# A windowed-attention and mixture-of-experts kernel: one written order for five sequencers, PSUM as eight named banks, shared own values in stage 1

## The chip, the cores and the metric

The kernel runs on one core of one Trainium2 chip. The metric is the device time of one execution in microseconds (us). The engines are TensorE (PE, its weight loads shown as PEld), VectorE (DVE), ScalarE (ACT), GpSimd (POOL) and SyncE (SP, which here only issues DMAs).

## The reference, cut to what matters

Two attention layers follow each other, for 8 batches of 576 positions.

```python
# stage 1: 8 heads of 64, each query sees the 64 positions up to itself
scores = (q @ k.transpose(0, 1, 3, 2)) / 8            # [8, 8, 576, 576]
mask = (rel >= 0) & (rel < 64)
x = softmax(where(mask, scores, -1e9)) @ v            # -> x [8, 576, 512]
# stage 2: 4 experts, each a causal attention with one head of 64; 2 experts per token by a gate
logits = x @ w_gate;  topk, w = best 2 of 4, softmax over the two
for e in range(4):
    q, k, v = x @ wq[e], x @ wk[e], x @ wv[e]
    ye = softmax(causal(q @ k.T / 8)) @ v @ wo[e]     # [8, 576, 512]
    out += (weight of e, 0 where e is not chosen) * ye
```

## The kernel before, in words

Stage 1 works on blocks of 64 positions; five units `d` per batch hold blocks 0-1, 2-3, 4-5, 6-7 and 8 (`UNITS`). `s1_mm` puts the scores of a unit into two PSUM banks, `s1_soft` makes the softmax in the tile `p1` of the unit: masked maximum on DVE (line 183, `tensor_tensor_reduce`, a custom instruction in the trace), exp on ACT (190), normalisation on POOL (198), 32x32 transposes on DVE (203). Stage 2 works on pairs of experts `pr`: `s2_v`, `s2_k`, `s2_q` are projections (lines 224 to 226: each product of fp32r parts is three matmuls), `s2_mm` the scores of half `x` of the rows (357), `s2_soft` and `s2_w` their softmax in `P2[pr]` (375, 379, 418), `s2_turn` the transposes (433), `s2_gate` the gate, `s2_o` the output projection with its copy (595) and store.

Both value products are one routine, `av`: 32x64 tiles of the array, four row groups `r` and two column groups `c`, all matmuls at line 528. A joint call takes the 18 key groups of one `(b, pr)` of stage 2 and units of stage 1 of batch `b+2`: units 0, 1 with `pr` 0, units 2, 3, 4 with `pr` 1. For batches 0 and 1 each unit has a call of its own (`EARLY`). In stage 1 a block `k` takes the values of its own block and of the one before; the first block of a unit needs extra steps, "edge", because its probabilities of the block before lie in its own tile and can't ride with the step "own" of that block, as they do inside a unit (`m` 2: one matmul of 64 columns). Each product of fp32 operands stands in the trace as two matmuls with a weight load each. The result is evicted by pairs: ACT copies to the fp32r high part (554), DVE subtracts it for the low part (555). The stage-2 values come from `VR`, one tile, filled by `s2_rep` with 24 DMAs (16 of `VN`, 8 of `V8`) for each `(b, pr)`, which can start when the `av` before has read `VR`. The values of stage 1 are loaded by `load_v`, 16 DMAs for each third of a batch.

PSUM holds one buffer of four banks, tag `a`, which `s2_mm` (both halves) and `av` take in turn, and four buffers of one bank, tag `s`, for all else (`s1_mm` takes two).

`put` gives each routine a time in units of half a batch, from tables (`EARLY`, `S1POS`, `BPOS`, `APOS`, `POS`, `WPOS`). The calls are sorted by it. Up to 1.0 and from 15.5 on the framework's scheduler orders all engines; between, PE keeps the sorted order (`manual_schedule`) and the framework orders DVE, ACT, POOL and SP.

Of the kernel before, what the change touches and what calls it, by code (L numbers as in the profile page):

```python
# [25 lines left out]
P1BUFS = 4  # L26
EARLY = ((-0.9, -0.7), (-0.8, -0.5), (-0.65, -0.35), (-0.5, -0.2), (-0.35, -0.1),
         (-0.2, 0.1), (0.0, 0.35), (0.3, 0.6), (0.5, 0.8), (0.7, 0.95))
S1POS = (0.04, 0.69, 0.04, 0.38, 0.69)
BPOS = (0.05, 0.7)  # L30
APOS = 0.4
POS = {"KQ1": (-0.2, 0.95), "O": (0.45, 1.3), "V": (-0.5, 0.2), "G": (0.2, 0.2), "KQ0": (0.2, 0.95), "V8": (0.45, 0.55)}
WPOS = (-0.7, -0.3, -0.2, 0.4)
FIXED = (1.0, 15.5)
# [3 lines left out]
def window_attention_moe_attention(ctx: ExitStack, tc: tile.TileContext, qT, kT, vW,  # L38
# [5 lines left out]
    psum = ctx.enter_context(tc.tile_pool(name="psum", bufs=2, space=PSUM))  # L44
# [6 lines left out]
    def banks(name, tag, n=1):  # L51
        return psum.tile([128, n, 512], F32, tag=tag, bufs=1 if tag == "a" else 4, name=name)
# [84 lines left out]
    def split_weights(i):  # L137
# [5 lines left out]
        yield "lo"  # L143
# [10 lines left out]
    S1, P1 = {}, {}  # L154

    def s1_mm(b, d):
        k0, k1 = UNITS[d]
        ps = [psum.tile([128, 2, 2, 128], F32, tag="s", bufs=4, name=f"s1_{b}_{d}_{x}") for x in range(2)]
# [14 lines left out]
    def s1_soft(b, d):  # L173
# [4 lines left out]
        pt = work.tile([128, 2, NP, 128], F32, tag="p1", bufs=P1BUFS, name=f"p1_{b}_{d}")  # L178
        yield "ttr"
        for k in range(n):  # L180
            for p in range(NP):
                own = 64 if k0 + k == 0 else 0
                nc.vector.tensor_tensor_reduce(out=pt[:, k, p, own:], in0=ps[p % 2][:, k, p // 2, own:],  # L183
                                               in1=win[:, own:], scale=-0.125, scalar=3.0e38, op0=OP.add, op1=OP.min,
                                               accum_out=st[:, 0, k, p:p + 1])
        yield "exp"
        for k in range(n):
            for p in range(NP):
                own = 64 if k0 + k == 0 else 0
                nc.scalar.activation(pt[:, k, p, own:], pt[:, k, p, own:], AF.Exp, bias=st[:, 0, k, p:p + 1],  # L190
                                     scale=-1.0, accum_out=st[:, 1, k, p:p + 1])
        yield "norm"
        nc.vector.tensor_scalar_add(st[:, 2, :n], st[:, 1, :n], 1e-9)
        nc.vector.reciprocal(st[:, 2, :n], st[:, 2, :n])  # L194
        for k in range(n):
            for p in range(NP):
                own = 64 if k0 + k == 0 else 0
                nc.gpsimd.tensor_scalar(pt[:, k, p, own:], pt[:, k, p, own:], st[:, 2, k, p:p + 1], 1.0,  # L198
                                        op0=OP.mult, op1=OP.mult)
        yield "turn"  # L200
        for k in range(n):
# [26 lines left out]
    def s2_v(b, j):  # L228
        if j < 4:
            need(("x", b, j), ("w", "v"))  # L230
        else:
            need(("x", b, 4), ("x", b + 1, 4))
        ps = psum.tile([128, 512], F32, tag="s", bufs=4, name=f"v2ps_{b}_{j}")
# [6 lines left out]
        yield "v"  # L240
# [24 lines left out]
    def s2_gate(b, j0, j1):  # L265

        n = j1 - j0
        need("late", *(("v", b, j) for j in range(j0, j1)))
# [4 lines left out]
        tc.keep_in_program_order(nc.vector.tensor_tensor(g4[:, 0], lf, le, op=OP.is_gt))  # L273
# [8 lines left out]
        nc.vector.tensor_sub(gt[:, 1], lg, gs[:, 0, :, None].to_broadcast([128, n, E]))  # L282
# [80 lines left out]
    def s2_soft(b, pr, x):  # L363
# [17 lines left out]
        for k, parts in enumerate(SCORES[x]):  # L381
            for i, key, n, at in parts:
                if i == 1:
                    n = 192
# [350 lines left out]
```

## Time and profile before

| what | value |
|---|---|
| median of 3 runs | 783.1 us (780.98 to 784.85) |
| profiled execution: its own time | 782.28 us |
| its span, first to last instruction | 780.5 us |
| mean granted TensorE clock, as a share of 2.4 GHz | 0.782 |
| busy: PE, PEld, DVE, ACT, POOL | 539.0, 484.1, 406.0, 290.1, 189.7 us |
| first joint `av` starts / last one with stage-1 units ends | 148.3 us / 670 us |

A busy share is an average over stages. PE's time is the span less its idle time, and the idle time has a releaser: what ended it. "issue" as a releaser means that PE waited for nothing that the profile shows.

### The profile page before, as it was taken

What the parts mean: (1) busy time and instruction counts of PE and PEld (TensorE: products, weight loads), DVE (VectorE), ACT (ScalarE), POOL (GpSimd) and SP (SyncE); (2) the same over time, 40 slices, a digit from 0 to 9 for tenths busy, and PEclk for the clock granted to TensorE, in tenths of its full rate; (3) what the DMA queues carried; (4) which work ended last, traced back from release to release, by engine and by line L of the source; (5) the groups of instructions that cost most, each with busy time, mean ns of one, the idle gap of its engine ahead of it and who ended that gap; (6) DMA issues with size and microseconds to landing.
All of it is one profiled execution on the core that took longest, in us unless ns stands there. A gap on an engine that the chain in (4) does not pass through costs nothing.

```text
span 780.5 us, 30957 instructions
## 1 busy us (share of the span) xinstructions
PE 539.0 (69%) x13006; PEld 484.1 (62%) x13006; DVE 406.0 (52%) x1813; ACT 290.1 (37%) x1162; POOL 189.7 (24%) x470
## 2 busy tenths in 40 slices
PE   3358759676596765968478766787578756698775
PEld 2257648566585654857366666766567656587564
DVE  2545546846157362674427563565625844376542
ACT  3334535534135341534215351443504523234210
POOL 2421413423024030241303321032312312021120
PEclk9566778876588695988769685796858878699877
DMA  5654342134343313433235232443324121122332
GB/s 157 190 157 122 85 126 79 44 79 117 80 127 103 106 32 82 134 97 86 78 89 153 72 91 52 112 118 76 107 61 138 58 49 32 32 84 58 85 86 69
DMA packets 81884, 72.30 MB, mean 93 GB/s; under 512 B 14416, under 2 KB 68688, under 8 KB 81744
## 3 DMA queue, kind: packets, MB, share of 16 engines
q1 hardware_dynamic: 81664, 70.19, 33.0%
q8 instruction: 102, 1.67, 0.9%
q14 instruction: 38, 0.31, 0.1%
q10 hardware_dynamic: 80, 0.13, 0.0%
HBM read 41.95 MB, written 9.44 MB: 66 GB/s over the span
## 4 chain that ended last, share of the span: by engine, by line
PE 42%; DVE 15%; issue 13%; ACT 13%; POOL 10%; SPq 4%; DMA 3%; POOLq 0%; ACTq 0%; DVEq 0%
PE o L528 20%; POOL p L198 8%; ACT p L190 8%; DVE p L375 3%; PE s L168 3%; DVE p L433 2%; SPq L82 2%; PE s L357 2%; DVE p L203 2%; DMA k<-in_kT_dram 2%; ACT p L379 2%; PE qps L224 2%; PE kps L224 2%; PE kps L225 2%; PE kps L226 2%
## 5 line engine op out<-in xcount | busy, mean ns | idle before, releaser
L198 POOL TENSOR_SCALAR p<-p,st 128x128 f32<-128x128 f32 (+1 forms) x288 | 99.0, 366 | 291.9 <-DVE st L194 127.7
L528 PE MATMUL o<-p,v 32*64 32x32 f32 (+1 forms) x5504 | 95.4, 279 | 96.2 <-issue 68.2
L528 PEld LDWEIGHTS o<-p,v 32*64 32x64 f32 x5504 | 88.0, 188 | 101.8 <-issue 82.3
L190 ACT ACTIVATE p<-p,st 128x128 f32<-128x128 f32 (+1 forms) x288 | 110.1, 384 | 68.0 <-DVE st L183 62.6
L528 PE MATMUL o<-p,vr 32*64 32x128 f32 (+3 forms) x4224 | 86.6, 302 | 63.3 <-DVE r L375 37.4
L528 PEld LDWEIGHTS o<-p,vr 32*64 32x64 f32 x4224 | 79.8, 166 | 70.1 <-issue 66.2
L554 ACT ACTIVATE xh<-o 128x128 fp32r<-128x128 f32 (+3 forms) x88 | 30.2, 343 | 217.6 <-PE o L528 184.5
L555 DVE TENSOR_TENSOR xl<-o,xh 128x128 fp32r<-128x128 f32 (+3 forms) x88 | 32.7, 371 | 134.0 <-ACT xh L554 133.9
L379 ACT ACTIVATE p<-p,r 128x192 f32<-128x192 f32 (+3 forms) x128 | 77.4, 605 | 65.7 <-DVE r L375 46.1
L418 POOL TENSOR_SCALAR p<-p,r 128x192 f32<-128x192 f32 (+3 forms) x128 | 72.7, 586 | 89.1 <-DVE r L414 65.8
L203 DVE STREAM_TRANSPOSE p<-p 128x512 f32<-128x512 f32 (+1 forms) x72 | 49.1, 682 | 71.7 <-POOL p L198 71.7
L168 PE MATMUL s<-k,q 64*64 64x128 f32 (+1 forms) x1152 | 57.3, 327 | 28.5 <-DVE logits L247 18.4
L433 DVE STREAM_TRANSPOSE p<-p 128x320 f32<-128x320 f32 (+3 forms) x112 | 67.0, 621 | 15.5 <-POOL p L418 14.3
L183 DVE CUSTOM_DVE_ANT_0 p<-s,win 128x128 f32<-128x128 f32 (+1 forms) x288 | 65.4, 277 | 14.5 <-PE s L168 14.4
L375 DVE CUSTOM_DVE_ANT_0 p<-s,causal 128x320 f32<-128x320 f32 (+3 forms) x160 | 67.0, 465 | 7.4 <-PE s L360 4.4
L168 PEld LDWEIGHTS s<-k,q 64*64 64x64 f32 x1152 | 42.7, 167 | 38.1 <-DVE logits L247 19.8
L357 PE MATMUL s<-kt,qt 64*128 64x256 f32 (+2 forms) x480 | 47.0, 336 | 20.1 <-DVE st L194 10.1
L357 PEld LDWEIGHTS s<-kt,qt 64*128 64x128 f32 x480 | 37.2, 198 | 27.7 <-issue 25.8
L190 ACT ACTIVATION_READ_ACCUMULATOR p<-p,st 128x1 f32 x288 | 53.9, 187 | 0.0
L224 PE MATMUL qps<-xh,wqhi 128*128 128x320 f32 (+1 forms) x128 | 46.5, 363 | 0.5 <-issue 0.5
L224 PE MATMUL kps<-xh,wkhi 128*128 128x320 f32 (+1 forms) x128 | 44.3, 346 | 0.0
L225 PE MATMUL qps<-xl,wqhi 128*128 128x320 f32 (+1 forms) x128 | 43.1, 337 | 0.0
(106 smaller groups left out, 1039.9 us busy)
## 6 DMA issues: line engine op xcount, KB each, us to landing
v<-in_vW_dram SPq DMA_DIRECT2D x384, 48.0 KB, 1.9
vr<-vn SPq DMA_DIRECT2D x256, 64.0 KB, 2.5
q<-in_qT_dram SPq DMA_DIRECT2D x24, 384.0 KB, 3.5
k<-in_kT_dram SPq DMA_DIRECT2D x16, 512.0 KB, 4.6
out_dram<-out SPq DMA_DIRECT2D x32, 256.0 KB, 2.1
k<-in_kT_dram SPq DMA_DIRECT2D x8, 384.0 KB, 4.9
vr<-v SPq DMA_DIRECT2D x128, 16.0 KB, 1.8
out_dram<-out SPq DMA_DIRECT2D x7, 128.0 KB, 2.5
```

What stands on the lines that cost most here:

```text
L168: nc.tensor.matmul(ps[p % 2][o:o + 64, k - k0, p // 2, own:], lhsT=QC[b, c][r, p, at:at + 64], rhs=KC[b, c][r, p, at + own:at + 128], star ...
L183: nc.vector.tensor_tensor_reduce(out=pt[:, k, p, own:], in0=ps[p % 2][:, k, p // 2, own:], in1=win[:, own:], scale=-0.125, scalar=3.0e38, ...
L190: nc.scalar.activation(pt[:, k, p, own:], pt[:, k, p, own:], AF.Exp, bias=st[:, 0, k, p:p + 1], scale=-1.0, accum_out=st[:, 1, k, p:p + 1])
L198: nc.gpsimd.tensor_scalar(pt[:, k, p, own:], pt[:, k, p, own:], st[:, 2, k, p:p + 1], 1.0, op0=OP.mult, op1=OP.mult)
L203: nc.vector.transpose(pt[:, k, :, own:], pt[:, k, :, own:])
L224: nc.tensor.matmul(ps, lhsT=ah, rhs=bh, start=first, stop=False)
L357: nc.tensor.matmul(ps[:, 2 * k + e, at:at + n], lhsT=QT[pr][r, w, q], rhs=KT[b, pr][r, m, key:key + n], start=y == 0, stop=y == 2)
L375: nc.vector.tensor_tensor_reduce(out=dst, in0=src, in1=mask, scale=1.0, scalar=3.0e38, op0=OP.add, op1=OP.min, accum_out=to)
L379: nc.scalar.activation(p, p, AF.Exp, bias=r2[:, 0, y:y + 1], scale=-1.0, accum_out=r2[:, 1, y:y + 1])
L418: nc.gpsimd.tensor_scalar(p, p, r2[:, 3, x:x + 1], 1.0, op0=OP.mult, op1=OP.mult)
L433: nc.vector.transpose(P2[pr][:, c], P2[pr][:, c])
L528: nc.tensor.matmul(to, lhsT=lhsT, rhs=rhs, start=first[r, c] == i, stop=last[r, c] == i, skip_group_check=True)
```

## The change

All calls and their steps stand in one string, `ORDER`, of 1991 words; each word runs a unit of work to its next `yield`, and the digits behind a colon are the PSUM banks that the step takes. DVE, ACT, POOL and SP follow this order too. PSUM is one tile `PS` of eight banks; `av` takes four neighbouring ones, `s2_mm` is split and takes two at a time. The softmax routines yield after each block or row group; `s2_soft` takes in what `s2_w` and `s2_turn` did. `P1` is one tile for the nine blocks of a batch, and `av` merges neighbouring units, so that "edge" stands only at the first block of a run; the units of batch 1 go in two calls (0, 1 and 2, 3, 4) in place of five. In `av` the row group now turns fastest. Two of five output copies go to ACT (`OUTS`). The words `l`, `q`, `h`, `r` are loads of weights, of queries and keys, of values, and the fill of `VR`; `m`, `s` stage 1; `v`, `k`, `j`, `g`, `x`, `y`, `o` stage 2 (`j` is `s2_q`, `y` the softmax); `a`, `e` are `av`. The order below is that around the joint calls of batch 3; the rest of the string is alike.

```diff
+OUTS = (1, 0, 1, 0, 1)
+EARLY = ((0, (0,)), (0, (1,)), (0, (2,)), (0, (3,)), (0, (4,)), (1, (0, 1)), (1, (2, 3, 4)))
+ORDER = (
+    'l1 l1 l0 l0 f f c c q00 q00 l2 l2 w1 w1 w1 q01 q01 w0 l3 l3 h00 h00 w0 w0 m00:45 m00 s00 s00 s00 w2 w2 w2 s00 '
...
+    'k401:2 o23 y310 v42 s54 s54 o23 o23 s53 y310 a30:4 v42 v42 g40 y310 s53 y310 y310 g40 s52 y310 r310 r310 y310 '
+    'y310 s52 s53 g40 g40 s53 r311 r311 j401:0 s53 a30 s53 a30 a30 a30 a30 h60 h60 k400:1 s53 s53 j401 a30 a30 a30 '
+    'j401 j401 a30 v50:3 s52 k400 a30 s52 k401 k400 k400 a30 a30 a30 m60:01 m60 a30 a30 k401 k401 v50 s52 a30 a30 '
+    'v50 v50 x4001:26 x4001 s52 s60 x4000:34 x4000 s52 s52 s60 s60 x3111:57 x3111 s60 j411:0 y311 y400 y311 y400 '
+    'j410:1 y400 j411 k410:3 j410 y311 j411 j411 y400 y311 j410 j410 y311 y311 m61:01 m61 k410 q62 q62 a31:4 y400 '
+    'k410 k410 s61 y400 s61 s60 s61 y400 s60 r400 r400 s61 y400 y400 s61 y400 y400 s61 y400 h61 h61 y400 y400 '
+    'x4100:01 x4100 s61 a31 a31 a31 v51:2 a31 s60 a31 s61 h62 h62 a31 a31 k411:3 a31 v51 s61 s61 a31 a31 k411 v51 '
+    'v51 s60 a31 v52:2 a31 a31 a31 a31 s60 s60 a31 a31 a31 k411 k411 v44:4 y410 v52 v52 v52 y410 o33:5 v44 v44 v44 '
+    'r401 r401 g44 x4101:46 x4101 g44 g44 g44 x4010:70 x4010 x4011:12 x4011 v53:3 y401 y401 m62:70 m62 v53 y410 y401 '
+    'm63:12 m63 q70 q70 v53 v53 s62 o31:3 y410 y401 s62 y401 y410 o32:4 y401 y401 y410 o30:0 s63 s62 y410 o30 y410 '
+    's63 j500:6 o31 o30 o30 s62 y410 o31 o31 a40:0 g50 y410 j500 o32 o33 s62 o32 o32 y410 g50 s62 s63 o33 o33 y410 '
...
-    psum = ctx.enter_context(tc.tile_pool(name="psum", bufs=2, space=PSUM))
+    psum = ctx.enter_context(tc.tile_pool(name="psum", bufs=1, space=PSUM))
-    def banks(name, tag, n=1):
-        return psum.tile([128, n, 512], F32, tag=tag, bufs=1 if tag == "a" else 4, name=name)
+    PS = psum.tile([128, 8, 512], F32, name="ps")
+    banks = []
+    def bank():
+        return PS[:, banks.pop(0)]
...
+    P1 = const.tile([128, BLK, NP, 128], F32, name="p1")
-        pt = work.tile([128, 2, NP, 128], F32, tag="p1", bufs=P1BUFS, name=f"p1_{b}_{d}")
...
-    def s2_mm(b, pr, x):
-        ps = SB[b, pr, x] = banks(f"s2_{b}_{pr}_{x}", "a", 4)
+    def s2_mm(b, pr, x, k):
+        ps = SB[b, pr, x, k] = [bank() for e in range(2)]
...
-        o = banks(f"o_{name}", "a", 4)
+        first = banks.pop(0)
+        o = PS[:, first:first + 4]
...
             for kj in range(18):
                 at = 4 * (kj % 4) + kj // 4 if kj < 16 else kj
-                for r in range(4):
-                    i = max(1, (kj + 5 - r) // 4)
-                    for c in range(2):
+                for c in range(2):
+                    for r in range(4):
+                        i = max(1, (kj + 5 - r) // 4)
...
+        for b1, k0, k1 in marks:
             for s in range(2):
-                steps = []
+                steps = [(k0, "edge")] if k0 else []
                 for k in range(k0, k1):
-                    own = [(k, 1, "own"), (k, 1, "over")] if k == k1 - 1 else [(k, 2, "own"), (k, 1, "over")]
-                    steps += own
-                    if k > k0 or k0:
-                        steps += [(k, 1, "past")] + ([(k, 1, "edge")] if k == k0 else [])
+                    steps += [(k, "own"), (k, "whole")]
...
+                            elif what == "own":
+                                v, t = values(b1, k, p, r, half), t[:, 64 + 32 * half:96 + 32 * half]
+                                if k < k1 - 1:
+                                    n = 2
+                                    t = bass.AP(t.tensor, offset=t.offset, ap=[list(t.ap[0]), [448, 2], [1, 32]])
...
                 nc.scalar.activation(hi, src, AF.Copy)
+                yield
                 nc.vector.tensor_sub(lo, src, hi)
+                yield
...
+    units = {}
+    def unit(name, f, *args):
+        def steps():
+            r = f(*args)
+            if r is not None:
+                yield from r
+        units[name] = steps()
...
+            ds = () if b + 2 >= NB else (2, 3, 4) if pr else (0, 1)
+            unit(f"a{b}{pr}", av, (b, pr), tuple((b + 2, d) for d in ds))
...
+    with tc.manual_schedule(engines={getattr(mybir.EngineType, x) for x in ("PE", "DVE", "Activation", "Pool", "SP")}):
+        for x in ORDER.split():
+            x, _, y = x.partition(":")
+            banks[:] = map(int, y)
+            next(units[x], None)
```

## Rows read from the trace of the kernel before

**Rows 1.** The page, part 1: busy time, share of the span, instructions.

```profile
span 780.5 us, 30957 instructions
PE 539.0 (69%) x13006; PEld 484.1 (62%) x13006; DVE 406.0 (52%) x1813; ACT 290.1 (37%) x1162; POOL 189.7 (24%) x470
```

**Rows 2.** Busy time by stretch: length, each engine's busy time, clock, DMA share, GB/s.

```profile
0.00:148.30 148.30, 89.51 (x2060) 79.39 (x2060) 76.32 (x393) 63.96 (x289) 46.40 (x131) 0.77 0.47 125
148.30:698.40 550.10, 392.15 (x9622) 355.40 (x9622) 287.39 (x1276) 205.40 (x806) 128.86 (x312) 0.77 0.32 87
698.40:780.50 82.10, 57.31 (x1325) 49.30 (x1324) 42.32 (x146) 20.74 (x68) 14.46 (x27) 0.86 0.27 74
```

**Rows 3.** Waits of PE, 148.3 to 698.4 us: total us, times, longest.

```profile
PE o L528 <- issue: 66.1, 42, 2.5
PE o L528 <- DVE r L375: 33.2, 6, 8.0
PE s L168 <- DVE logits L247: 18.4, 5, 4.0
PE v2ps L224 <- POOL x8h L559: 12.1, 3, 4.1
```

**Rows 4.** Timeline of PE, one joint `av`: start, us, what, [idle before].

```profile
378.26 0.77 PE L528 MATMUL o<-p,vr 32*64 32x128 f32 x16 [8.04 <-DVE r L375]
...
386.81 1.90 PE L528 MATMUL o<-p,v 32*64 32x32 f32 x128 [2.08 <-issue]
390.26 2.37 PE L528 MATMUL o<-p,v 32*64 32x32 f32 x128 [1.56 <-issue]
394.27 1.84 PE L528 MATMUL o<-p,v 32*64 32x32 f32 x106 [1.64 <-issue]
```

**Rows 5.** The page, part 3, the instruction queue: packets, MB, share.

```profile
q8 instruction: 102, 1.67, 0.9%
```

**Rows 6.** Line 528, matmuls of stage 1: durations min/median/max, first and last start.

```profile
L528 PE MATMUL o<-p,v x5504: 184/289/365, 15.3 to 670.1; 32*64 32x32 f32 x156, 32*64 32x64 f32 x41
```

**Rows 7.** By stretch as in Rows 2: projections of 256 columns, twice.

```profile
396.84:398.55 1.71, 1.71 (x10) 1.71 (x10) 0.82 (x2) 0.44 (x1) 0.00 (x0) 0.50 0.06 13
705.94:707.14 1.20, 1.20 (x13) 1.20 (x11) 0.67 (x3) 0.66 (x3) 0.00 (x0) 1.00 0.04 7
```

**Rows 8.** Timeline of ACT and DVE: the first evictions of that `av`.

```profile
396.20 0.44 ACT L554 ACTIVATE xh<-o 128x320 fp32r<-128x320 f32 x1 [16.77 <-PE o L528]
396.67 0.49 DVE L555 TENSOR_TENSOR xl<-o,xh 128x320 fp32r<-128x320 f32 x1 [12.27 <-ACT xh L554]
397.20 0.44 ACT L554 ACTIVATE xh<-o 128x320 fp32r<-128x320 f32 x1 [0.56 <-DVE xl L555]
```

**Rows 9.** Timeline of SP's queue: runs of DMA issues (L262 `VR`; L82 values).

```profile
382.61 12.60 SPq L262 DMA_DIRECT2D vr<-vn  x16
...
398.25 8.64 SPq L82 DMA_DIRECT2D v<-in_vW_dram  x16
...
414.25 8.46 SPq L82 DMA_DIRECT2D v<-in_vW_dram  x16
```

**Rows 10.** Stage-2 softmax by line and form: total us, mean ns, then idle.

```profile
L375 DVE CUSTOM_DVE_ANT_0 p<-s,causal 128x320 f32<-128x320 f32 x64 | 28.7, 476 | 3.0 <-PE s L357 2.9
...
L379 ACT ACTIVATE p<-p,r 128x576 f32<-128x576 f32 x32 | 24.6, 769 | 19.4 <-DVE r L399 19.4
...
L433 DVE STREAM_TRANSPOSE p<-p 128x576 f32<-128x576 f32 x32 | 23.8, 769 | 8.4 <-POOL p L418 8.4
...
L418 POOL TENSOR_SCALAR p<-p,r 128x576 f32<-128x576 f32 x32 | 23.5, 747 | 89.1 <-DVE r L414 65.8 <-PE s L360 12.3 <-DVE st L183 11.0
```

**Rows 11.** Timeline of SP's queue at the start.

```profile
1.78 8.22 SPq L82 DMA_DIRECT2D v<-in_vW_dram  x16
...
20.66 0.69 SPq L133 DMA_DIRECT2D p<-in_wv_dram  x1
```

**Rows 12.** Timeline of PE: its first matmuls.

```profile
6.03 2.41 PE L168 MATMUL s<-k,q 64*64 64x64 f32 x48 [6.03 <-DMA k<-in_kT_dram]
```

More of the change, by code (lines that the diff above doesn't have):

```diff
@@ L267, in s2_gate @@
         n = j1 - j0
-        need("late", *(("v", b, j) for j in range(j0, j1)))
+        need("late", *(("logits", b, j) for j in range(j0, j1)))
         lg = L[b % 2][:, j0:j1]
@@ L305, in proj @@
         n = 64 * (b1 - b0)
-        ps = psum.tile([128, 512], F32, tag="s", bufs=4, name=f"{name}ps_{b}_{pr}_{half}")
+        ps = bank()
         w = slice(128 * pr, 128 * pr + 128)
@@ L420, in s2_turn @@
[L420 to L433 removed]
+        need(("g", b, 0), *([("g", b & ~1, 4)] if x else []))
@@ new lines, in s2_soft @@
+        for i in rows:
+            if i == 1:
+                py = PY[b, pr] = work.tile([64, 2, 64], F32, tag="py", bufs=2, name=f"py_{b}_{pr}")
+                for e in range(2):
+                    nc.vector.transpose(py[:, e], px[64 * e:64 * e + 64])
+            for e in range(1 if i == 3 else 2):
+                p = P2[pr][:, row(i, 1 if i == 3 else e):][:, :(64 + 128 * i) * (2 if i == 3 else 1)]
+                nc.vector.transpose(p, p)
+            if i > 2:
+                made.add(("t", b, pr, x))
+            yield
@@ L524, in av @@
+        opens, ends = {}, {}
         for i, (r, c, *_) in enumerate(ops):
-            first.setdefault((r, c), i)
-            last[r, c] = i
+            opens.setdefault((r, c), i)
+            ends[r, c] = i
         for i, (r, c, to, lhsT, rhs) in enumerate(ops):
-            nc.tensor.matmul(to, lhsT=lhsT, rhs=rhs, start=first[r, c] == i, stop=last[r, c] == i,
+            nc.tensor.matmul(to, lhsT=lhsT, rhs=rhs, start=opens[r, c] == i, stop=ends[r, c] == i,
                              skip_group_check=True)
-        yield "evict"
+        if s2:
+            made.add(("av", *s2))
@@ L531, in av @@
+        made.update(("x", b1, d) for b1, d in units)
+        yield
         jobs = []
@@ L668, in window_attention_moe_attention @@
-    put(1.2, s2_rep, 0, 0, 0)
-    put(1.8, s2_rep, 0, 0, 1)
-    assert not joined, joined
-    order.sort(key=lambda x: x[:2])
-    left = [(t, f, args) for t, _, f, args in order]
-    E_ = mybir.EngineType
-    for t1, engines in ((FIXED[0], None), (FIXED[1], {E_.PE}), (99, None)):
-        with tc.manual_schedule(engines=engines) if engines else nullcontext():
-            while left and left[0][0] < t1:
-                _, f, args = left.pop(0)
-                for _ in f(*args) or ():
-                    pass
+            unit(f"m{b}{d}", s1_mm, b, d)
```

376 lines of the change are left out of this document (153 added, 223 removed), and 74 rows, old and new, of the table ORDER.

## The prediction, made before the changed kernel ran

> **What bounds the kernel now.** I read the busy times first: PE is busy for 539 of 780.5 us, and no other engine comes near it [rows 1]. So the question is what PE's idle 241 us are. I cut the span at the starts of the joint `av` calls: a head of 148.3 us, a steady stretch of 550.1 us with twelve of them (six batches, 91.7 us each), and a tail of 82.1 us [rows 2]. In the steady stretch PE is busy for 392.2 us and idle for 158. Its waits say why: 66 us are "issue", and nearly all the rest, 92 us, are waits for other engines, of which the largest is `av` waiting for the masked reads of stage 2 (L375), 33.2 us in six waits [rows 3].
>
> Two things are to be seen in one `av` [rows 4]. It stands idle for 8.04 us until the last read of line 375: the scores and `av` share the single four-bank buffer. Then, once under way, it runs exactly 128 matmuls, stops, runs 128, stops: starts at 386.81, 390.26 and 394.27, 3.45 and 4.01 us apart, so 3.73 us for 128 matmuls, though these execute in 1.9 to 2.4 us. 128 matmuls with their weight loads are 256 instructions, and the instruction queue moves 1.67 MB in 102 packets, 16 KB each [rows 5], or 64 bytes for each of 256. So I read "issue" as PE waiting for its next instructions: there a matmul costs 29.1 ns whatever it computes, and in this part only the number of matmuls counts.
>
> **The change part by part. (1) Shared own values.** Inside a run of units "edge" goes. It is 8 calls for each of two halves `s`, and each call is two matmuls of the trace: 32 for each seam, one seam in units 0, 1 and two in units 2, 3, 4. So 96 matmuls go in each of the batches 1 to 7, 672 of 5504 [rows 6], and 576 of these lie in the steady stretch. At 29.1 ns that is 16.8 us; the 96 of batch 1 I take at half of it, 1.4 us, in the head. Bounds: execution alone (1.90 us for 128, 14.8 ns, from the fastest run of 128 in rows 4) gives 8.5 us for the 576; 29.1 ns each is the top. The Trainium skill ("Runtime: NRT & Kernel Launch", Instruction fetch mechanics) says that crossing a 16 KiB block is "mostly hidden"; by that the 576 would be worth 8.5 us and the sum below 8 us more. This trace does not agree: gaps of 1.56 to 2.08 us stand at every 128th matmul [rows 4].
>
> **(2) Eight named banks.** Before, both halves of the scores and `av` passed one buffer, and PE's fixed order could not go round a wait. Now a half of the scores takes two banks at a time, and the order can put projections between. What is left I read from the order by what PE has between a hand-over's two ends. First, from the last scores of a pair to its `av` (`x3111` to `a31`): two reads of up to 0.48 us, two exps of 0.77, two scalings of 0.75 and two transposes of 0.77 [rows 10], some 0.5 us of small steps, and three reads-in-pairs of `y400` queued between on DVE, taken as 3 us: 9 us. PE has `j411 j410 k410 m61` there: three projections of twelve matmuls at 0.12 us (clock at 1.00 of 2.4 GHz) to 0.21 us (0.50, which is 1.2 GHz) [rows 7], that is 4.3 to 7.6 us, and about 1 us for `m61`. Between 0.4 and 3.7 us are not covered. Second, from the end of `av` to its readers: ACT and DVE take turns on the same banks, one job each 1.0 us [rows 8], eight jobs, so 8 us; PE has `x4100 v51 k411 v52` there, 5.5 to 8.8 us with 1.2 for the scores: up to 2.5 us open. With two hand-overs of each kind in a batch, at 1.6 us each, 6.5 us a batch stay, 39 us of the 92. So 53 us go. Bounds: 20 us (only six tenths of the 33.2 us of the shared buffer) and 85 us (7 left).
>
> **(3) The written order of DVE, ACT, POOL.** In `s2_soft` the exp of `px` now stands first on ACT and needs the last read, so the first exp comes about 2 us later than before; it is hidden, since `y` of half 0 is due one `av` earlier than it is used. Two of five output copies on ACT are hidden too: DVE and ACT are busy for 52% and 37% [rows 1]. The row group turning fastest I cost at nothing: in the part where instructions come at 29.1 ns, execution (14.8 to 18.5 ns) has room [rows 4]; were that cover gone, every ns more per matmul would be some 9 us over all 9250.
>
> **(4) SP.** `r` (24 DMAs into `VR`) needs the read of `VR` by the `av` before; it was issued 4.35 us after that `av` began and took 12.6 us for 16 DMAs; 16 loads of values take 8.64 and 8.46 us [rows 4, 9]. In the written order the second part of `r` for even batches stands behind both value loads: `a31`, `r400`, `h61`, `h62`, `r401`, `a40`. That is 4.35 + 12.6 + 8.64 + 8.46 + some 5 for the eight of `r401` + 2 for landing = 41 us from one `av` to the next, against a mean of 45.8 now (550.1 / 12) and 39.3 that the other terms leave. So SP is next in line, and sets a floor for such an interval: three of the twelve lose about 1.7 us each. I put 5 us for it in the sum, bounds 0 and 15. Elsewhere both parts of `r` come first, 24 us, and are hidden.
>
> **(5) The clock.** Right after an `av` with its gaps projections run at 0.50, later at 1.00 [rows 7]; the steady stretch has a mean of 0.77 [rows 2], so the lower level for 46% of it. A batch has 177 projection matmuls (`k` and `j` 96, `v` 54, `o` 27), 1062 in six; at 0.09 us each, all that now run at the lower level (46%) cost 44 us more than at the higher. Fewer waits will win some of that back, but the stretch behind each `av` stays: I take 8 us, bounds 0 and 44.
>
> **(6) Head and tail.** Now the first queries are issued at once and PE begins at 6.03 us [rows 12]; the weights follow from 20.66 us [rows 11]. The new order issues weights first: some nine issues of about 0.65 us each [rows 11], so PE begins 5 us later. What follows has fewer waits; PE is idle for 59 us of the head [rows 2], and I take 10 us of them as won. With the 1.4 us of (1): head −6, bounds −18 and +7. The tail is a chain of `av`, `r`, `av` with 16 issues of some 12 us each [rows 9], which the change leaves: −2, bounds −10 and +2.
>
> **The sum.** Steady: 550.1 − 16.8 − 53 + 5 − 8 = 477, or 79.5 us a batch. Head 142, tail 80: 699, and the profiled execution has 1.8 us outside its span (782.28 against 780.5): 701. That execution lies 0.8 us under the median of 783.1, so I predict **701 us**, a ratio of about 0.895.
>
> With all terms at their ends: 550.1 − 16.8 − 85 − 44 = 404, 130 and 72 give 608 us; 550.1 − 8.5 − 20 + 15 = 537, 155 and 84 give 778. So many terms won't fall on one side: the forecast's own range is 650 to 750.
>
> **Rivals.** *A, the waits come back under another name (slower).* Every queue keeps the written order, so a late step holds all behind it. `a30` needs the banks of `s52`, and the order puts five groups of reads (`s52 s53 s54`, in DVE's queue behind `y310` and `y311`) before it. If durations differ from those the order was written for, each joint `av` waits for the last read, as it does now for 8.04 us [rows 4], but all twelve, not six: 12 × 8.04 = 96 us where I left 39 and won 53. From about 7 us a call more than I reckoned (82 / 12) the change gains nothing; at 8.04 more it is 701 + 96 = 797. For it: DVE is 52% busy [rows 1], and ACT stands for 16.77 us at the eviction already [rows 8], with all that is queued behind. Against: the written order has 5 to 9 us of PE work at each of these places. The Trainium skill ("TensorE: Matmul & The Clock Gate", Architectural detail) calls ACT's and DVE's queues strict FIFO, which is this mechanism; the 16.77 us agree with it. *B, only the matmul count counts.* The waits for other engines come from the softmax chain, not from banks, and keep their 92 us: 782.3 − 18 = 764. For it: nine tenths of the named releasers are DVE, ACT or POOL steps [rows 3]; against, the wait on L375 goes with its buffer. *C, instructions are hidden once PE's other waits go:* the 576 are worth 8.5 us, 709; little for it, since the gaps stand inside one unbroken `av`. The Trainium skill's section named under (1) has this as its rule. *D, no change:* SP is the bound. Its order makes each interval 41 us or more only where loads precede `r`; for no change every interval would have to stay at 45.8, which needs 5 us more in all twelve: 783.
>
> **How the numbers follow.** Within 0.5% (4 us) a measurement of this kernel, whose runs lie 3.9 us apart, can't tell a change from none. Chances: the forecast (650 to 750) 0.70; below it, 0.04; B and what lies between 750 and 779, 0.08; C 0.03; D 0.04; A and slower 0.11. Faster: 0.85, the same 0.04, slower 0.11. For 8 in 10 the range goes from 640 to 765: it leaves out A, D, the upper part of B and a little below.
>
> **What would show it.** Line 528 of stage 1 with 4832 matmuls, still in runs of 128 with gaps; joint `av` calls of 516 and 628; waits of `av` for line 375 gone; a start-to-start of two `av` of about 79 us; SP's `r401` landing just before `a40`. The prediction is wrong if `av` still waits for DVE by several us each time, if PE's other waits stay near 92 us, if `av` gets slower per matmul by the new turn of row groups, or if SP's loads hold `r` back in every interval.

## The result and the profile after

The kernel now takes 707.9 us in the median of four runs (705.4 to 710.7) against 782.4 before: a ratio of 0.905, with a 95% interval of 0.900 to 0.909. The prediction was 701 us, from 640 to 765. The profiled execution after took 705.4 us, with a span of 703.6. Ratios, here and below, leave out executions over 1.5% slower than the fastest of the same kernel (three in all) and medians don't, so the two can differ by some tenths of a per cent.

Busy times, the page's part 1, then the shares of the chain of work that ended last, part 4, by engine and by line:

```profile
span 703.6 us, 29613 instructions
PE 512.4 (73%) x12334; PEld 456.5 (65%) x12334; DVE 392.6 (56%) x1785; ACT 286.5 (41%) x1166; POOL 190.6 (27%) x470
...
PE 51%; issue 12%; SPq 8%; DMA 4%; DVE 1%; ACT 0%; ACTq 0%; DVEq 0%
PE ps L606 16%; PE ps L311 9%; PE ps L312 8%; PE ps L313 8%; PE ps L445 6%; SPq L166 5%; PE ps L253 3%; DMA k<-in_kT_dram 2%; SPq L349 2%; SPq L347 2%; DMA out_dram<-out 2%; PE ps L448 1%; DMA vr<-v 0%; DVE out L665 0%; DVE p L460 0%
```

The same shares of the kernel before, part 4 of its page:

```profile
PE 42%; DVE 15%; issue 13%; ACT 13%; POOL 10%; SPq 4%; DMA 3%; POOLq 0%; ACTq 0%; DVEq 0%
```

PE lost 672 matmuls [rows 1]. The chain tells more: DVE, ACT and POOL held 38% of it and now 1%. SP's queue has doubled its share, and one line of it, L166, the loads of values, has 5%, some 35 us.

Busy time by stretch, cut as in [rows 2] at the starts of the joint `av` calls (columns: length; busy time and instructions of PE, PEld, DVE, ACT, POOL; clock, DMA share, GB/s):

```profile
0.00:135.20 135.20, 87.98 (x2016) 77.86 (x2016) 76.72 (x413) 64.61 (x295) 46.16 (x127) 0.80 0.54 143
135.20:622.40 487.20, 369.55 (x9033) 331.55 (x9032) 282.25 (x1253) 202.19 (x809) 134.79 (x325) 0.78 0.35 94
622.40:703.60 81.20, 54.83 (x1289) 47.09 (x1288) 33.64 (x121) 19.74 (x63) 9.70 (x19) 0.82 0.30 85
```

| stretch | before | predicted | after |
|---|---|---|---|
| head | 148.3 | 142 | 135.2 |
| steady, six batches | 550.1 | 477 | 487.2 |
| tail | 82.1 | 80 | 81.2 |

PE's waits in the steady stretch (total us, times, longest), to be laid beside [rows 3]:

```profile
PE ps L606 <- issue: 77.5, 43, 4.7
PE ps L253 <- DMA k<-in_kT_dram: 20.8, 2, 10.8
PE ps L253 <- DVE out L665: 15.2, 2, 10.3
PE ps L311 <- DVE m L460: 1.4, 3, 0.6
```

PE is idle for 117.65 us there (487.20 − 369.55), where it was 158. Of these 77.5 are issue; 40 are waits for others, as many as the prediction left (39), but other ones. The waits for softmax steps, evictions and banks are down from 89 to 4 us (the 92 of before had one wait for keys in them, 2.9 us). In their place stand two waits for loads of keys, 20.8 us, and two for output copies, 15.2 us. No wait of `av` for line 460 (375 before) is left.

What a load of keys waits for is seen in the timeline of SP's queue before the longest of them (start, us, what), and then in that of PE:

```profile
470.49 11.13 SPq L349 DMA_DIRECT2D vr<-vn  x16
481.66 5.57 SPq L347 DMA_DIRECT2D vr<-v  x8
487.32 7.61 SPq L166 DMA_DIRECT2D v<-in_vW_dram  x16
495.02 0.39 SPq L151 DMA_DIRECT2D q<-in_qT_dram  x1
495.46 0.51 SPq L152 DMA_DIRECT2D k<-in_kT_dram  x1
```

```profile
500.05 1.13 PE L253 MATMUL ps<-k,q 64*64 64x128 f32 x16 [10.79 <-DMA k<-in_kT_dram]
```

The load is a single DMA whose issue takes half a microsecond, and its pair of issues stands behind 40 others that take 24.5 us. The copy into `out` waits for the DMA that writes out the tile's former content (38.3 us on DVE in the whole run, 27.8 on ACT), and that one stands in the same queue: before the longest such wait, three writes are issued at 209.54 us, behind two loads of values and one of queries and keys that fill the queue from 191.80.

Inside an `av`, the runs of 128 are still there (timeline of PE, to be laid beside [rows 4]):

```profile
430.60 2.16 PE L606 MATMUL ps<-p,v 32*64 32x64 f32 x128 [1.41 <-issue]
434.61 2.21 PE L606 MATMUL ps<-p,v 32*64 32x32 f32 x128 [1.85 <-issue]
438.61 0.43 PE L606 MATMUL ps<-p,v 32*64 32x32 f32 x6 [1.79 <-issue]
438.97 1.81 PE L445 MATMUL ps<-kt,qt 64*128 64x256 f32 x12
```

Starts stand 4.01 and 4.00 us apart, and 128 matmuls execute in 2.2 us. Line 606 has 4832 of them on stage-1 values, as said.

### The profile page after: what moved, and what is told of

Its sections match the earlier page's. It is cut to its first block, busy times and chain, and to the rows that moved or that the text cites. A ratio compares the mean times of both kernels' runs of the same rounds, so it can differ in the third digit from the quotient of the medians.

```text
span 703.6 us, 29613 instructions
## 1 busy us (share of the span) xinstructions
PE 512.4 (73%) x12334; PEld 456.5 (65%) x12334; DVE 392.6 (56%) x1785; ACT 286.5 (41%) x1166; POOL 190.6 (27%) x470
## 2 busy tenths in 40 slices
DMA packets 81878, 72.20 MB, mean 103 GB/s; under 512 B 14416, under 2 KB 68688, under 8 KB 81744
## 3 DMA queue, kind: packets, MB, share of 16 engines
q8 instruction: 96, 1.57, 1.0%
## 4 chain that ended last, share of the span: by engine, by line
PE 51%; issue 12%; SPq 8%; DMA 4%; DVE 1%; ACT 0%; ACTq 0%; DVEq 0%
PE ps L606 16%; PE ps L311 9%; PE ps L312 8%; PE ps L313 8%; PE ps L445 6%; SPq L166 5%; PE ps L253 3%; DMA k<-in_kT_dram 2%; SPq L349 2%; SPq L347 2%; DMA out_dram<-out 2%; PE ps L448 1%; DMA vr<-v 0%; DVE out L665 0%; DVE p L460 0%
## 5 line engine op out<-in xcount | busy, mean ns | idle before, releaser
L606 PE MATMUL ps<-p,v 32*64 32x32 f32 (+1 forms) x4832 | 87.9, 288 | 68.4 <-issue 59.1
L505 POOL TENSOR_SCALAR p<-p,r 128x320 f32<-128x320 f32 (+3 forms) x128 | 73.0, 586 | 213.1 <-DVE r L500 76.8
L606 PEld LDWEIGHTS ps<-p,v 32*64 32x64 f32 x4832 | 79.7, 192 | 75.8 <-issue 68.9
L606 PE MATMUL ps<-p,vr 32*64 32x128 f32 (+3 forms) x4224 | 75.5, 264 | 44.0 <-issue 32.4
L606 PEld LDWEIGHTS ps<-p,vr 32*64 32x64 f32 x4224 | 67.9, 140 | 50.6 <-issue 36.2
L253 PE MATMUL ps<-k,q 64*64 64x128 f32 (+1 forms) x1152 | 48.7, 315 | 64.9 <-DMA k<-in_kT_dram 48.3
L460 DVE CUSTOM_DVE_ANT_0 p<-ps,causal 128x320 f32<-128x320 f32 (+3 forms) x160 | 67.8, 471 | 34.6 <-PE ps L445 24.3
L635 DVE TENSOR_TENSOR xl<-ps,xh 128x256 fp32r<-128x256 f32 (+3 forms) x76 | 27.8, 399 | 100.7 <-ACT xh L633 100.3
L464 ACT ACTIVATE p<-p,r 128x576 f32<-128x576 f32 (+3 forms) x128 | 77.1, 605 | 8.5 <-DVE r L488 8.4
L266 DVE CUSTOM_DVE_ANT_0 p<-ps,win 128x128 f32<-128x128 f32 (+1 forms) x288 | 62.2, 277 | 32.3 <-PE ps L253 32.2
L517 DVE STREAM_TRANSPOSE p<-p 128x192 f32<-128x192 f32 (+3 forms) x112 | 63.0, 610 | 3.4 <-POOL p L505 2.8
L445 PE MATMUL ps<-kt,qt 64*128 64x320 f32 (+2 forms) x480 | 59.6, 381 | 3.5 <-issue 1.7
L445 PEld LDWEIGHTS ps<-kt,qt 64*128 64x128 f32 x480 | 42.4, 226 | 13.6 <-issue 4.5
```

The lines of the kernel that those rows point to most:

```text
L253: nc.tensor.matmul(ps[p % 2][o:o + 64, k - k0, p // 2, own:], lhsT=QC[b, c][r, p, at:at + 64], rhs=KC[b, c][r, p, at + own:at + 128], star ...
L266: nc.vector.tensor_tensor_reduce(out=P1[:, k0 + k, p, own:], in0=ps[p % 2][:, k, p // 2, own:], in1=win[:, own:], scale=-0.125, scalar=3.0 ...
L445: nc.tensor.matmul(ps[e][:, at:at + n], lhsT=QT[pr][r, w, q], rhs=KT[b, pr][r, m, key:key + n], start=y == 0, stop=y == 2)
L460: nc.vector.tensor_tensor_reduce(out=dst, in0=src, in1=mask, scale=1.0, scalar=3.0e38, op0=OP.add, op1=OP.min, accum_out=to)
L464: nc.scalar.activation(p, p, AF.Exp, bias=r2[:, 0, y:y + 1], scale=-1.0, accum_out=r2[:, 1, y:y + 1])
L505: nc.gpsimd.tensor_scalar(p, p, r2[:, 3, 2 * i - 1 + e:2 * i + e], 1.0, op0=OP.mult, op1=OP.mult)
```

## The experiments

Two ideas run through the twelve kernels: that `av` goes at the pace at which instructions arrive, so that only the number of matmuls counts, and that SP's queue is now the next in line. Medians are us; the ratio is to the kernel before, run on the same chip, with its 95% interval. Chips differ a little: the kernel before took 782.4 us beside after, 784.3 beside e1, e2, e3 and e5, 787.2 beside e4, e6, e7 and e8, 782.8 beside e9 and e10, and 787.3 beside e11 and e12.

| kernel | median | ratio | interval |
|---|---|---|---|
| after | 707.9 | 0.905 | 0.900 to 0.909 |
| e1_edges | 726.8 | 0.929 | 0.924 to 0.933 |
| e2_columns | 707.4 | 0.901 | 0.897 to 0.906 |
| e3_values_one | 655.3 | 0.836 | 0.832 to 0.839 |
| e5_pe_sp | 741.9 | 0.945 | 0.940 to 0.950 |
| e4_before_values_one | 769.5 | 0.978 | 0.971 to 0.986 |
| e6_q_first | 707.8 | 0.895 | 0.887 to 0.902 |
| e7_edges_pe_sp | 751.9 | 0.955 | 0.950 to 0.960 |
| e8_one_q_first | 660.5 | 0.838 | 0.832 to 0.844 |
| e9_weave | 771.4 | 0.988 | 0.977 to 0.998 |
| e10_half_columns_b | 711.7 | 0.911 | 0.902 to 0.920 |
| e11_weave | 661.7 | 0.841 | 0.839 to 0.843 |
| e12_edges_pe | 747.5 | 0.946 | 0.941 to 0.951 |

### e1_edges: the 672 matmuls back, all else as after

```diff
-        for b1, k0, k1 in marks:
+        for b1, (k0, k1) in [(b1, UNITS[d]) for b1, d in units]:
```

> The changed kernel with its stage-1 products cut at every unit again: 672 matmuls more in line 606, nothing else changed. Theory 1 (instructions arrive at a fixed pace in av, 29.1 ns for a matmul and its weight load): +16 to +20 us, about 726 us, the steady av calls back to 548 and 692 matmuls and longer by 0.9 and 1.9 us. Rival (the gaps are hidden, only execution counts, 14.8 ns): +8 to +10 us, about 717. Rival 2 (SP's queue sets the end, so PE's work is covered): no change, 708.

It was 18.9 us slower than after (726.76 − 707.88), or 28.1 ns for each of the 672 matmuls. But the stretches don't share it out like the matmuls, of which 96 lie in the head and 576 in the steady stretch. Head and steady stretch of e1, then PE's longest waits in the steady one:

```profile
0.00:146.07 146.07, 91.62 (x2112) 80.97 (x2112) 76.56 (x413) 64.61 (x295) 46.36 (x127) 0.78 0.53 139
146.07:641.37 495.30, 372.94 (x9607) 334.52 (x9606) 281.03 (x1253) 201.84 (x809) 135.29 (x325) 0.79 0.34 91
```

```profile
PE ps L606 <- issue: 89.5, 48, 3.9
PE ps L253 <- DMA k<-in_kT_dram: 17.3, 2, 10.4
PE ps L253 <- DVE out L665: 8.3, 2, 7.8
```

In the steady stretch the price on PE is as reckoned: issue rises by 12.0 us (89.5 against 77.5) and PE's busy time by 3.4, together 15.4 us or 27 ns for each of the 576. The stretch itself is only 8.1 us longer, since the waits for keys and output copies give back 10 us. The other 10.9 us stand in the head, where 96 matmuls at 29 ns would be 2.8; why the head grew by so much more was not tried. A profile is one execution: after, e2 and e6, which have the same matmuls, have heads of 135.0 to 135.8 us and steady stretches of 484.9 to 487.2, but e10 has 137.6 and 494.0. So the 10.9 us are clear of this, and the 8.1 are known to some us.

The kernel before had as many matmuls as e1 and only 66.1 us of issue in its steady stretch: a part of what the other waits gave up comes back as waits for instructions.

### e2_columns: the row group turns slowest again

```diff
-                for c in range(2):
-                    for r in range(4):
-                        i = max(1, (kj + 5 - r) // 4)
+                for r in range(4):
+                    i = max(1, (kj + 5 - r) // 4)
+                    for c in range(2):
...
-                    for c in range(2):
-                        for r in range(4):
+                    for r in range(4):
+                        for c in range(2):
```

> The changed kernel with the column group turning fastest in av, as before the change. Theory: instructions set the pace in av, so no change within 0.5%, 704 to 712. Rival: the new turn is worth something of its own; if each of the 9250 matmuls got 2 ns slower, 726.

707.44 against 707.88, and ratios whose intervals overlap: the turn of the row groups makes no difference that can be seen here.

### e3_values_one: values loaded by one DMA in place of 16

```diff
-        for par in range(2):
-            src = vW[NP * b + par:NP * b + NP:2, 64:128].rearrange("p (x r) (h c) -> r p x h c", x=2, h=2)
-            for r in range(4):
-                for x in range(2):
-                    nc.sync.dma_start(v_t[32 * r:32 * r + 32, par::2, x, :n],
-                                      src[:, :, x, (r // 2) ^ par, 64 * b0:64 * b1])
+        nc.sync.dma_start(v_t[:, :, :, :n], vW[b, :, :, :, 64 * b0:64 * b1])
```

For it the input of values is laid out in another order in memory.

> The changed kernel with each third of a batch of stage-1 values loaded by one DMA in place of 16 (the input laid out for it), so SP issues 360 DMAs less, about 170 us of its 491 us. Theory 2 (SP's queue is the bound that took over): the waits of the stage-1 scores for keys (48 us) and of the output copies for a free tile go, and the time falls by 35 to 55 us, to 655 to 673. Rival (PE's own work and the pace of its instructions bind, waits only change name): a fall under 15 us, 693 or more.

655.3 us, 52.6 less than after and the fastest of all. DMA issues of the page of after, then of e3 (KB each, us from issue to landing):

```profile
v<-in_vW_dram SPq DMA_DIRECT2D x384, 48.0 KB, 1.9
```

```profile
v<-in_vW_dram SPq DMA_DIRECT2D x24, 768.0 KB, 6.7
```

The same bytes come with 360 issues fewer, and SP's issuing time falls from 490.7 to 318.8 us, 0.48 us an issue. A DMA now takes 6.7 us to land in place of 1.9, but what stands behind it no longer waits for 16 issues. The first two stretches of e3, then PE's waits in its steady one:

```profile
0.00:119.90 119.90, 82.23 (x2016) 73.00 (x2016) 76.13 (x413) 64.58 (x295) 46.32 (x127) 0.96 0.59 169
119.90:571.60 451.70, 361.40 (x9031) 324.32 (x9030) 282.31 (x1253) 202.09 (x809) 135.22 (x325) 0.81 0.35 100
```

```profile
PE ps L601 <- issue: 73.5, 43, 2.3
PE ps L248 <- DMA k<-in_kT_dram: 8.7, 2, 5.5
PE ps L248 <- DVE out L660: 3.2, 2, 2.8
```

The steady stretch is 35.5 us shorter: 12.1 from waits for keys, 12.0 from output copies, 4.0 from issue and 8.1 from PE's busy time, the clock being 0.81 in place of 0.78. The head is 15.3 us shorter, with a clock of 0.96 in place of 0.80. The Trainium skill ("DMA: Bandwidth & Descriptors", Rules for kernel authors) advises to coalesce small transfers, since under 64 KB one pays mostly overhead. The runs agree for loads of 48 KB, with one addition: what they paid was not the bandwidth of these loads but the time for which the queue kept others waiting. A rival is that the other layout makes the transfers lighter: it brings fewer small packets (8656 under 512 B, where after has 14416). But a load of keys does not land sooner by it: 512 KB take 6.5 us from issue to landing, against 5.2 after.

### e4_before_values_one: the same edit on the kernel before

> The kernel before the change with each third of a batch of stage-1 values loaded by one DMA in place of 16, as in e3_values_one. Theory 2 (before, other waits of TensorE hid SP's queue; the change uncovered it): little, 0 to -2%, 768 to 784. Rival (SP's issue time was a bound all along and the change only left it there): a fall like that of e3_values_one, by 35 us or more, to 748 or less.

769.5 against 787.2 us: 17.7 us, a third of what it brings after. Head and steady stretch:

```profile
0.00:135.09 135.09, 84.64 (x2061) 74.92 (x2061) 76.06 (x393) 63.88 (x289) 47.57 (x131) 0.85 0.51 145
135.09:680.98 545.89, 392.90 (x9623) 356.89 (x9623) 286.50 (x1276) 205.03 (x806) 128.79 (x312) 0.77 0.30 85
```

In the profiles the steady stretch gains 4.2 us (550.1 to 545.9), where e3 gained 35.5. There `av` still waits for the softmax step of line 375 (renumbered 370 in this kernel; 42.5 us in the whole run, 37.4 before). So in the steady stretch SP's queue is a bound that the change made. In the head it was one already: 13.2 us of the gain lie there (148.3 to 135.1), about as much as the 15.3 of e3.

### e5_pe_sp: DVE, ACT and POOL not held to the written order

```diff
-    with tc.manual_schedule(engines={getattr(mybir.EngineType, x) for x in ("PE", "DVE", "Activation", "Pool", "SP")}):
+    with tc.manual_schedule(engines={getattr(mybir.EngineType, x) for x in ("PE", "SP")}):
```

> The changed kernel with only PE and SP kept in the written order; the framework's scheduler orders DVE, ACT and POOL, as before the change. Theory 3 (the gain comes from the banks and from PE's order): within 1.5% of 708, 697 to 719. Rival (the written order of DVE, ACT and POOL carries a good part of the 75 us): 730 to 760, with waits of av and of the scores for DVE back.

741.9 us, slower than after by 34 us in the medians and 32 in the ratios. PE's waits, whole run (issue is 81.1 here):

```profile
PE ps L253 <- DMA k<-in_kT_dram: 54.4, 8, 13.7
PE ps L253 <- DVE out L665: 21.4, 2, 11.5
PE ps L606 <- DMA vr<-vn: 11.1, 4, 5.9
PE ps L606 <- DVE out L665: 10.0, 2, 8.1
```

Output copies cost 31.4 us in place of 15.2, the fill of `VR` 11.1 in place of 3.5, keys 54.4 in place of 48.3. The head is 13.7 us longer than after and the steady stretch 21.6. So the order of the small steps on DVE, ACT and POOL is a part of the gain of its own.

### e6_q_first and e8_one_q_first: queries before weights, on after and on e3

```diff
-    'l1 l1 l0 l0 f f c c q00 q00 l2 l2 w1 w1 w1 q01 q01 w0 l3 l3 h00 h00 w0 w0 m00:45 m00 s00 s00 s00 w2 w2 w2 s00 '
+    'q00 q00 l1 l1 l0 l0 f f c c l2 l2 w1 w1 w1 q01 q01 w0 l3 l3 h00 h00 w0 w0 m00:45 m00 s00 s00 s00 w2 w2 w2 s00 '
```

> The changed kernel with the first load of queries and keys moved ahead of the weights in the written order. Theory: the first matmul starts at about 6 us and not at 11.8, but the head is set later, by the 16-DMA value loads on SP, so 0 to -2 us, 706 to 708. Rival (the late start goes through to the end, the 5 us of the prediction): 702.

> e3_values_one with the first load of queries and keys ahead of the weights. Theory: now that SP's queue is short in the head, the earlier start of TensorE goes through: 4 to 6 us less than e3_values_one, 649 to 651. Rival (weights are then late for the first projections): no change, 655.

Neither moved the time clear of noise: 707.8 against 707.9, and 660.5 against 655.3. The ratios of e8 and e3 overlap (0.832 to 0.844, 0.832 to 0.839); those of e6 and after (0.895 and 0.905) just do, and leave room for a gain. The profiles show none: the head is 135.0 us in e6 against 135.2, and 123.2 in e8 against 119.9. First the first matmul of after, then the first two of e6:

```profile
11.76 1.56 PE L253 MATMUL ps<-k,q 64*64 64x64 f32 x32 [11.76 <-DMA k<-in_kT_dram]
```

```profile
6.09 1.55 PE L253 MATMUL ps<-k,q 64*64 64x64 f32 x32 [6.09 <-DMA k<-in_kT_dram]
15.29 3.89 PE L253 MATMUL ps<-k,q 64*64 64x128 f32 x64 [7.64 <-DVE st L266]
```

PE begins 5.67 us sooner and then stands 7.64 us at the next scores, which are ready no earlier; in e8 it begins at 6.04 and then waits 7.78.

### e7_edges_pe_sp and e12_edges_pe: fewer parts still

e7 is e1 with the edit of e5; e12 holds PE alone to the order:

```diff
-        for b1, k0, k1 in marks:
+        for b1, (k0, k1) in [(b1, UNITS[d]) for b1, d in units]:
...
-    with tc.manual_schedule(engines={getattr(mybir.EngineType, x) for x in ("PE", "DVE", "Activation", "Pool", "SP")}):
+    with tc.manual_schedule(engines={getattr(mybir.EngineType, x) for x in ("PE",)}):
```

> The changed kernel with the edges back at every unit and only PE and SP in the written order: what is left of the change are the eight banks and the order of PE and SP. If the parts add up: 707.9 + 18.9 + 34.0 = 761, 21 us under the kernel before. If the extra matmuls are covered by the waits that the framework's order brings: 742 to 750. If the banks and PE's order do nothing alone: 782.

> The changed kernel with the edges back at every unit and only PE in the written order; the framework orders DVE, ACT, POOL and SP as before. What is left are the eight banks with PE's order. If SP's written order is worth nothing: that of e7_edges_pe_sp, 752 within 1%. If SP's written order carries part of that gain: 760 to 784. If the written order of SP does harm: below 745.

The banks and PE's order alone, with the smaller edits that the change needs for them (split scores, one `P1`, two of five copies on ACT), give 0.946 (e12). The steady stretch of e12, and the largest wait in it that is not issue, keys, or output copies:

```profile
152.25:658.50 506.25, 377.57 (x9607) 336.97 (x9606) 275.54 (x1254) 202.35 (x799) 129.99 (x309) 0.79 0.33 88
```

```profile
PE ps L311 <- DVE m L460: 2.1, 4, 0.7
```

It is 43.8 us shorter than before, with 11.6 us of waits for softmax steps, evictions and banks (by my sum) where it was 89; waits for output copies are 22.5 us in it. Its head gains nothing (152.3 against 148.3).

SP's order adds nothing: with it the ratio is 0.955, and the two intervals just overlap. DVE's, ACT's and POOL's order brings it to 0.929 (e1), the shared values to 0.905 (after). The parts don't add up freely. The shared values are worth 18.9 us where all queues are ordered and some 8 where three are not (0.955 − 0.945 of 785). In the steady stretch they are worth nearly the same in both, 8.1 us (e1 to after) and 9.3 (e7 to e5): matmuls that PE runs in place of a wait for something else are cheap. The two cases differ in the head, by 10.9 and 2.6 us.

### e9_weave and e11_weave: `av` cut, with other work between, on e3

If instructions arrive at a pace of their own, work with longer matmuls between pieces of an `av` should let them run ahead. Both kernels cut the joint calls and put projections and scores of the order between; e11 moves the cuts behind the part that reads `VR`. Shown are the cuts, of e9 first and then of e11; the moved words of the order are left out:

```diff
+            if s2 and units and i + 1 in (120, 184, 248, 312)[:len(ops) // 64]:
+                yield
...
+            if s2 and units and i + 1 in (110, 174, 238)[:len(ops) // 100]:
+                yield
```

In e9 the cuts stand in the part that reads `VR`, and the fill of `VR` comes between, so that a part of its stage-2 products uses the values of the next fill.

> e3_values_one with the joint av calls cut after 240 matmuls and then every 128, and up to three of the TensorE steps that follow each call (scores and projections whose inputs and banks are ready, 26 in all) moved into the cuts. Theory 1 (the gaps are instructions on their way, and matmuls that run long for their number of instructions can fill them): issue waits fall from 92 us by 25 to 45 us, the time by 15 to 35 us against e3_values_one, to 620 to 640. Rival (the gaps belong to av itself, whatever runs before): issue waits stay and the time is that of e3_values_one, 655 within 1%.

> e3_values_one with the joint av calls cut after 220 matmuls and then at every 128th, and 19 neighbouring TensorE steps (18 projections or output products of 6 to 12 matmuls, one half of scores, that have their inputs and banks) moved into the cuts; the fill of VR and all loads stay behind the whole call, unlike e9_weave, where the fill stood inside it. Theory 1 (the gaps are instructions on their way, and a long matmul can run while they come): issue waits fall from 92 us by 15 to 30 us and the time by 10 to 25 us against e3_values_one, to 630 to 645. Rival (the gaps belong to av, or the steps moved were needed where they stood): 655 or more.

e9 tested something else than it should: PE's waits, whole run, are now those for that fill.

```profile
PE ps L598 <- DMA vr<-vn: 113.2, 36, 8.0
PE ps L598 <- issue: 41.4, 27, 2.7
```

e11 is clean of that. Its steady stretch, then PE's waits there:

```profile
117.50:575.00 457.50, 364.66 (x9056) 324.37 (x9056) 283.60 (x1268) 205.46 (x820) 137.04 (x329) 0.87 0.35 98
```

```profile
PE ps L597 <- issue: 49.7, 38, 2.6
PE ps L244 <- DMA k<-in_kT_dram: 18.0, 2, 10.2
PE ps L597 <- DVE r L451: 4.6, 3, 3.4
```

Issue falls from 73.5 to 49.7 us, as the idea says. But the stretch is no shorter (457.5 against 451.7): the wait for keys doubles, small waits for DVE, ACT and POOL come to some 19 us where e3 has 5 (by my sum), and the whole kernel stands at 0.841 against 0.836. So the 24 us were given back. That this is because the order around the cuts was not made again for the new due times is argued, not tried.

### e10_half_columns_b: half the columns, 16 in place of 32 and 32 in place of 64

```diff
-                                    t = bass.AP(t.tensor, offset=t.offset, ap=[list(t.ap[0]), [448, 2], [1, 32]])
+                                    t = bass.AP(t.tensor, offset=t.offset, ap=[list(t.ap[0]), [448, 2], [1, 16]])
...
-                            mm(r, c, place(r, c, spot[b1, k, s], spot[b1, k, s] + 32 * n), v, t)
+                            mm(r, c, place(r, c, spot[b1, k, s], spot[b1, k, s] + 16 * n), v, t if n == 2 else t[:, :16])
```

It computes the values of half the queries only, and clears the eight banks at the start (those lines are left out here).

> The changed kernel with half of the columns left out of each stage-1 matmul of av (the values of half the queries are not computed; PSUM is cleared once at the start), the number of matmuls unchanged. Theory 1 (the pace of instructions sets av's length): av calls and the time stay, 700 to 710, and the gaps get longer by what the matmuls get shorter. Rival (execution counts): 4832 matmuls shorter by some 5 to 7 ns each, 24 to 34 us less, 675 to 684.

711.7 us, no faster than after. One run of 128, to be laid beside those of after:

```profile
439.21 2.05 PE L608 MATMUL ps<-p,v 32*64 32x16 f32 x128 [1.71 <-issue]
```

So columns don't count, only matmuls. But it hardly tells the arrival of instructions from execution: the 18 runs of 128 on stage-1 values execute in 2.05 us on the mean, and in 2.20 after (both by my sum), so a matmul of half the columns is 1.2 ns shorter, and not the 5 to 7 that the rival needs. Between these two, e1 and e11 decide: in the steady stretch issue rises by 12 us with more matmuls and falls by 24 with other work between.

## Why the prediction was right, and where it was not

**The sum.** Its parts in the steady stretch, by the prediction's own steps:

| step | predicted | measured | from |
|---|---|---|---|
| (1) shared own values, 576 matmuls | −16.8 | −15.4 | PE's busy time and issue, e1 |
| (2) eight named banks | −53 | −85 | waits 89 to 4 us; to 12 in e12 |
| (4) SP | +5 | +33 | waits of 20.8 + 15.2 us, 2.9 before |
| (5) the clock | −8 | about −3 | below |
| issue that comes back | none | about +8 | the rest: 487.2 − (550.1 − 15.4 − 85 + 33 − 3) |
| steady | 477 | 487.2 | |

The total is near by luck: two errors of some 30 us, in (2) and in (4), stand against each other, and the head, 7 us shorter than forecast, takes up most of the 10 by which the steady stretch is longer.

**(1)** holds in its count (4832), in its runs of 128 with gaps and in its price on PE, 27 ns where 29.1 were forecast. What it is worth in time is another thing: the steady stretch of e1 is 8.1 us longer, not 16.8. That is rival C's figure (8.5 us for the 576, 709 in all), but not its reason: the instructions are not hidden, issue rises by 12.0 us, and other waits give way. The Trainium skill ("Runtime: NRT & Kernel Launch", Instruction fetch mechanics) calls the crossing of a 16 KiB block mostly hidden; 128 matmuls with their weight loads are such a block, the queue moves 1.57 MB in 96 packets, and here the blocks start 4.0 us apart for 2.2 us of work, so this trace does not agree.

**(2)** had the right mechanism and a term too small. The prediction left 1.6 us open at each of 24 hand-overs, reckoned from the work that PE has between; 4 us in all stayed, a little under the 7 that it gave as the lower bound. Rival A (a wait for the last read in each of twelve calls) did not come: there is no such wait. (The 16.77 us of rows 8, given for it, show ACT idle at an eviction, not that a step which was ready stood behind.) Rival B (the chain of softmax steps keeps its 92 us) is refuted by e12: with the banks and PE's order alone 12 of the 89 us are left. What e5 adds is that the written order of DVE, ACT and POOL, a part of the change that **(3)** costed only for what it might harm, is worth 34 us, in the steady stretch mostly by waits for output copies (15.2 us, and some 33 without it). The rest of (3), the turn of the row groups at nothing, holds (e2); line 606 has 9056 matmuls, not the 9250 reckoned with there.

**(4)** is the step that failed. That SP is next in line is right, but the place and the size are not. The prediction followed one step, `r401` before `a40`, and charged it, over three intervals, with 5 us. That step came as forecast, with 42.4 us from `a31` to `a40` and the last of `r401` landing at 462.7 us, where `a40` begins at 462.3, but it cost nothing: no `av` of the steady stretch waits for `VR` (5.9 us of such waits lie in the tail). It did not ask what else stands in the queue behind 16 issues of values: the loads of queries and keys for the scores of stage 1, one DMA each, and the output. These cost 36 us in the steady stretch, and the keys 27.5 more in the head (48.3 − 20.8; 6.0 before). e3 takes the 16 issues away and wins 52.6 us. Rival D (SP holds all twelve intervals at 45.8 us) is not what happened, the mean being 40.6 (487.2 / 12), but its engine was the right one to fear.

**(5)** took one row for a whole. It laid the 46% at the lower level, which it had from the mean clock of the stretch, on the projections; but before the change these ran at 0.88 on the mean (by my sum over the trace, as the other sums of this paragraph), with a quarter of them at the lower level. Projections do cost less after (0.91), but some of the stage-2 scores now stand right behind the gapped `av`, and pay. Line 357 before, line 445 after, the same 360 matmuls, in the steady stretch (length, PE busy, PEld busy, clock, DMA share, GB/s):

```profile
148.30:698.40 550.10, 34.13 (x360) 26.93 (x360) 0.77 0.32 87
```

```profile
135.20:622.40 487.20, 45.93 (x360) 33.10 (x360) 0.78 0.35 94
```

They cost 11.8 us more. 84 of the 360 come right behind an `av`, all of them at 0.50, where before none did; their mean clock goes from 0.97 to 0.82. The 2 us behind the `av` of the timeline above, most of them such scores:

```profile
439.00:441.00 2.00, 2.00 (x16) 1.67 (x14) 1.46 (x4) 1.60 (x4) 0.02 (x1) 0.50 0.44 109
```

Projections are down from 189.4 to 181.1 us, 8.3 us, which is the term that was predicted. With the scores of stage 1 6.5 us down, the three together are some 3 us less, not 8.

**(6)** The first matmul came at 11.76 us, as said, but the five microseconds by which the head was charged for it cost nothing (e6, e8). The head is 13.1 us shorter where 6 were forecast, and no run parts that gain: it is gone in e1, in e5 and in e12 (146.1, 148.9 and 152.3 us against 148.3). The tail is 0.9 shorter, where 2 were.

**What stays open.** The 8 us that came back lie in `av`: by my sum over its matmuls its busy time went from 132.9 to 113.8 us in the steady stretch, with 66.1 and 77.5 of issue, so 7.7 us in all where (1) is worth 15.4. That instructions have less time to run ahead, now that PE waits less for others, is argued and fits e11; it was not tried by itself. The banks and PE's new order were not tried apart. That a new written order on top of e11 keeps its 24 us was not tried, nor why the head answers so strongly to 96 matmuls.

## What to carry to other kernels

When an order on one engine removes its waits, list every queue that feeds it, and for each load ask what stands before it in that queue: one load cut into 16 issues cost more here, through loads behind it, than all hand-overs that remained. Where a matmul is short, count matmuls and not columns, and price one by taking a few hundred away, since its own duration was some six tenths of what it cost PE here. Read such a test by stretch and by waits: in the steady stretch shorter waits gave half of that price back, and the head hid this in the total. Parts of such a change are worth what the next bound lets them, so in the steady stretch the same edit brought 4.2 us before and 35.5 after.

## What the runs showed of the hardware

- Half the columns hardly count: the runs of 128 fp32 matmuls of 32x64 tiles on stage-1 values execute in 2.20 us on the mean with 32 and 64 columns (after) and in 2.05 with 16 and 32 (e10).
- Runs of 128 matmuls begin some 3.9 us apart whatever they compute (means of 3.81 before, 3.86 after, 3.93 in e1, 3.86 in e3, 3.83 in e10), about 30 ns for a matmul with its weight load.
- Behind such a gapped stretch the granted clock is at its lower level: 0.50, which is 1.2 of 2.4 GHz, from 439 to 443 us, though before that PE had stood only for the gaps of 1.4 to 1.9 us of the timeline above. In e11, with the gaps partly filled, the steady mean is 0.87 where it was 0.81 in e3.
- A DMA issue less frees SP's queue for 0.48 us, on the mean of the 360 that e3 saves ((490.7 − 318.8) / 360); the 24 that stay there take 0.72 us each for 16 times the bytes.
